# One column-tiled group for all logit sums of a block, and one pool of ten buffers for the products of both attention stages

## The chip, the cores and the metric

The kernel runs on one core of one Trainium2 chip. Its time is the device time of one execution in microseconds (us). A profiled execution has a span of its own, from its first to its last recorded instruction, which is a little shorter than the time of the run.

TensorE (PE) multiplies matrices, VectorE (DVE) does elementwise work and reductions, ScalarE (ACT) does functions and the copies from PSUM to SBUF, GpSimd (POOL) sets constants and takes powers, and SyncE (SP) issues all transfers.

## The reference

A transformer layer in which attention and feed-forward run side by side on the same normalised input: 2048 positions of 512 numbers, bf16.

```
xn  = layernorm(x)
out = x + A(xn) + B(xn)

A: q, k, v = xn @ wqkv, 32 heads of 16
   logits[h,s,w] = q[h,s] . k[h, s - 2*w] / 4     for w = 0..7 (masked below position 0)
   o[h,s] = sum over w of softmax(logits)[h,s,w] * v[h, s - 2*w]
   A = o @ wo
B: (gelu(xn @ w_gate) * (xn @ w_up)) @ w_down,    hidden width 1376
```

Each position looks at itself and at seven earlier ones, two apart. There is no dense product of queries and keys in it: logits are sums over 16 numbers of elementwise products, and so are the outputs over 8 weights.

## The kernel before

**Blocks.** The sequence is cut into four blocks of 512 positions, b = 0 to 3. For each block the kernel does, in this order of dependence: layer norm (L925 to L972) and a transpose of the result into `xnT`; the projections to q, k and v (L1045 for q and k of block 0, L1089 for the others; ACT copies them out at L1064, L1099, L1106, L1113); the logits; a softmax; the values' part; the feed-forward part (gate and up at L1305, gelu at L1315, the copy of up at L1322, their product on DVE at L1327 into `HT`); and the output (L1351 adds o @ wo, L1356 h @ w_down, in one PSUM bank; L1376 adds x).

**The logits.** The 512 channels are four groups g of 128, 8 heads each. For each g, DVE multiplies q by shifted keys, two times (wq = 0, 1), each for four of the eight shifts: a tensor of 128 x 2048 in bf16 (L1135), which goes to a buffer of the pool `PROD` (4 buffers of 4 KB per partition). TensorE then sums over the 16 channels of each head with a constant matrix `E8`: eight matmuls for one g (task `er`, L1151), each with 32 columns of weights, placed at `tile_position=(0, 32 * sj)`. That is the column-tiled mode, in which four matmuls of 32 columns stand side by side in the array. The windows of `E8` put each g on other rows, so that all four groups accumulate into one pair of PSUM banks (`lg`). The softmax (L1184 to L1214) starts when the fourth is done.

**The values' part.** The weights go through a scratch tensor in HBM (L1222 writes, L1229 reads into `PT`) and the values through another (L1120 writes, L1240 reads into `BS`). DVE multiplies them for each of four quarters dq in two halves (L1255), into the pool `PVS` (3 buffers of 8 KB, one for both halves). TensorE sums with the constant matrix `E4`, in the column-tiled mode as well, two quarters at a time: 16 matmuls (task `pvr`, L1274, `PVR_MERGE` = 2). ACT copies the sums to `OT` (L1285), which L1351 needs.

**The order of the work.** A planner writes it out before the kernel is built. Each task has an engine, a duration, what it reads and writes, and a priority (lower goes first). The planner goes through simulated time and gives each engine the most urgent task that is ready; it lets another task go first if that one fits in before. An item takes a buffer of its pool when its first task is placed, and gives it back when its last one is done. If no buffer is free, or the item's stream would be over its quota, the task can't be placed yet. The order of each engine is then fixed, and the engines wait for each other by semaphores. Lines that matter here:

```
sched = dict(PE_SLACK=1.6, DMA_BPUS=250e3,                         # L1387
             TOL=dict(pe=0.3, act=-0.3, dve=0.0, pool=-0.3, sp=0.0))
QUOTAS = dict(tp=2, qkv=2, lg=2, o=cfg.get("PVR_MERGE", 2), ffn=3, acc=2)   # L685
```

`PE_SLACK` is time that the planner leaves between the end of another engine's work and a TensorE task that waits for it. `QUOTAS` limits the PSUM banks (8 in all) by use. Feed-forward work has 3 banks, and four buffers each for the gate (`GG`) and up (`UU`) results, which come free when DVE has multiplied them (L1327). Priorities: logit products have base + 20 and value products base + 50, where base is 0, 700, 1400 and 2100 for the four blocks; feed-forward has 500 + 1000 b + j for its eleven column groups j. All transfers go through SP's one queue in planned order.

Of the kernel before, what the change touches and what calls it, by code (L numbers as in the profile page):

```python
# [638 lines left out]
BF = mybir.dt.bfloat16  # L639
# [24 lines left out]
def bass_parallel_sum__sliding_local_dilated__glu_gated_geglu__prompt_kernel(nc, A_x, A_wqkv, A_wo, B_x, B_w_gate, B_w_up, B_w_down, out, dbg=None, cfg=None):  # L664
    cfg = dict(cfg or {})
# [1 line left out]
    NSUBA = cfg.get("NSUBA", 1)  # L667
    NQT = cfg.get("NQT", 2)
    NXT = cfg.get("NXT", 3)
    NPROD = cfg.get("NPROD", 4)  # L670
    JA = cfg.get("JA", 8)
    NMS = cfg.get("NMS", 2)
    NDE = cfg.get("NDE", 1)
# [1 line left out]
    NPT = cfg.get("NPT", 2)  # L675
    NVT = cfg.get("NVT", 4)
    NBS = cfg.get("NBS", 3)
    NPVS = cfg.get("NPVS", 3)
    NOT = cfg.get("NOT", 2)
    NGG = cfg.get("NGG", 4)  # L680
    NHT = cfg.get("NHT", 2)
# [11 lines left out]
    PVR_MERGE = cfg.get("PVR_MERGE", 2)  # L693
# [11 lines left out]
    with contextlib.ExitStack() as es:  # L705
        block = es.enter_context(nc.Block())

        def sb(name, shape, dt):
            return es.enter_context(nc.sbuf_tensor(name, shape, dt))
# [10 lines left out]
        E8 = sb("E8", [128, 56], BF)  # L720
        E8f = sb("E8f", [128, 56], F32)
        E4 = sb("E4", [128, 32], BF)
# [11 lines left out]
        ms = sb("ms", [128, NMS, 3, 128], F32)  # L734
        XIN = sb("XIN", [128, NXIN, 2, 512], BF)
        QT = sb("QT", [128, NQT, 4, 512], BF)
        PROD = sb("PROD", [128, NPROD, 4, 512], BF)
        DE = sb("DE", [128, NDE, 1024], F32)
        PB = sb("PB", [128, NPB, 1024], BF)
        PT = sb("PT", [128, NPT, 1024], BF)  # L740
        VT = sb("VT", [128, NVT, 512], BF)
        BS = sb("BS", [128, NBS, 4, 514], BF)
        PVS = sb("PVS", [128, NPVS, 2, 4, 512], BF)
        OT = sb("OT", [128, NOT, 4, 512], BF)
        GG = sb("GG", [128, NGG, 512], BF)
        UU = sb("UU", [128, NGG, 512], BF)
# [3 lines left out]
        PS = es.enter_context(nc.psum_tensor("PS", [128, 4096], F32))  # L750
# [8 lines left out]
        G = Graph()  # L759
# [1 line left out]
        P_xin = Pool("xin", NXIN)  # L761
        P_xt = Pool("xt", NXT)
        P_qt = Pool("qt", NQT)
        P_prod = Pool("prod", NPROD)
        P_ms = Pool("ms", NMS)
        P_de = Pool("de", NDE)
        P_pb = Pool("pb", NPB)
        P_pt = Pool("pt", NPT)
        P_vt = Pool("vt", NVT)
        P_bs = Pool("bs", NBS)  # L770
        P_pvs = Pool("pvs", NPVS)
        P_ot = Pool("ot", NOT)
        P_gg = Pool("gg", NGG)
        P_uu = Pool("uu", NGG)
# [11 lines left out]
        I_E8 = Item("E8")  # L786
        I_E8f = Item("E8f")
        I_E4 = Item("E4")
# [21 lines left out]
            out=cf[:, :], in_=cf[:, :], pattern=[[-1, 128]], compare_op=ALU.is_equal, fill=0.0, base=0,  # L810
            channel_multiplier=1), rd=[I_cf], wr=[I_cf], prio=PC)
        G.task("pool", "c_idb", 0.65, lambda e: e.tensor_copy(out=ident[:, :], in_=cf[:, :]),
               rd=[I_cf], wr=[I_ident], prio=PC)
# [87 lines left out]
        for p in range(NP):  # L901
            b = p // 2
# [123 lines left out]
        for b in range(NB):  # L1026
# [98 lines left out]
                                   wr=[(I_VD, (b, g, hf))], prio=hb + 13, nbytes=128 * HWD * 2)  # L1125

            it_lg = Item("lg%d" % b, P_ps, "lg", width=2)
            for g in range(4):
                prs = []
                for wq in range(2):  # L1130
                    it_pr = Item("pr%d_%d_%d" % (b, wq, g), P_prod, "p")
                    prs.append(it_pr)

                    def mk_p(wq=wq, g=g, it=it_pr, itq=it_qt, c0b=c0b):
                        return lambda e: e.tensor_tensor(  # L1135
                            out=PROD[:, it.slot, :, :],
                            in0=bass.AP(QT, (itq.slot * 4 + g) * 512, [[NQT * 4 * 512, 128], [0, 4], [1, 512]]),
                            in1=bass.AP(KT, g * PITCH + 16 + c0b - 12 - 2 * wq, [[4 * PITCH, 128], [4, 4], [1, 512]]),
                            op=ALU.mult)
                    rdk = [(I_KT, (0, "t", t)) for t in range(4)] if b == 0 else [(I_KT, (b, g, 0))]  # L1140
                    rdk.append((I_KT, "pad") if b == 0 else (I_KT, (0, "t", 3)) if b == 1 else (I_KT, (b - 1, g, 0)))
                    rdq = [(it_qt, ("t", t)) for t in range(4)] if b == 0 else [(it_qt, (g, 0))]
                    G.task("dve", "pr%d_%d_%d" % (b, wq, g), d_dve(2048, 0.52), mk_p(),
                           rd=rdq + rdk, wr=[it_pr], prio=base + 20)

                def mk_r(g=g, prs=prs, lg=it_lg):
                    def f(e):
                        ins = None
                        for wq in range(2):
                            for sj in range(4):  # L1150
                                ins = e.matmul(  # L1151
                                    PS[32 * sj:32 * sj + 32, 512 * (lg.slot + wq):512 * (lg.slot + wq) + 512],
                                    lhsT=E8[:, 24 - 8 * g:56 - 8 * g],
                                    rhs=PROD[:, prs[wq].slot, :, sj * 128:(sj + 1) * 128],
                                    start=(g == 0), stop=(g == 3), tile_position=(0, 32 * sj))
                        return ins
                    return f
                G.task("pe", "er%d_%d" % (b, g), 0.46, mk_r(),
                       rd=prs + [I_E8] + ([it_lg] if g > 0 else []), wr=[it_lg], prio=base + 5, mode="c",
                       util=0.8)  # L1160

            it_pt = Item("pt%d" % b, P_pt, "pt")
            it_de = Item("de%d" % b, P_de, "de")
# [68 lines left out]
                   prio=base + 37, nbytes=256 * 1024)  # L1232

            it_ot = Item("ot%d" % b, P_ot, "ot")
            pvr_grp = []
            for dq in range(4):
                it_bs = Item("bs%d_%d" % (b, dq), P_bs, "bs")
                for j in (0, 2, 1, 3):
                    def mk_l(j=j, dq=dq, it=it_bs, c0b=c0b):
                        return lambda e: e.dma_start(  # L1240
                            BS[32 * j:32 * j + 32, it.slot, :, :],
                            bass.AP(VD, dq * 128 * PITCH + 16 + c0b - 2 - 4 * (3 - j),
                                    [[PITCH, 32], [32 * PITCH, 4], [1, 514]]))
                    rdv = [(I_VD, (b, g, hf)) for g in range(4) for hf in range(NHALF[b])]
                    if b > 0:
                        rdv += [(I_VD, (b - 1, g, NHALF[b - 1] - 1)) for g in range(4)]
                    else:
                        rdv.append((I_VD, "pad"))
                    G.task("sp", "ldb%d_%d_%d" % (b, dq, j), 0, mk_l(), rd=rdv, wr=[(it_bs, j)],
                           prio=base + 45, nbytes=int(1.8 * 32 * 4 * 514 * 2))  # L1250
                it_pv = Item("pv%d_%d" % (b, dq), P_pvs, "pv")
                for half in range(2):
                    def mk_pv(half=half, it=it_bs, ito=it_pv, itp=it_pt):
                        o = 2 - 2 * half
                        return lambda e: e.tensor_tensor(  # L1255
                            out=bass.AP(PVS, (ito.slot * 2 + half) * 2048,
                                        [[NPVS * 4096, 128], [512, 4], [128, 4], [1, 128]]),
                            in0=bass.AP(BS, it.slot * 4 * 514 + o,
                                        [[NBS * 4 * 514, 128], [514, 4], [128, 4], [1, 128]]),
                            in1=bass.AP(PT, itp.slot * 1024 + half * 128,  # L1260
                                        [[NPT * 1024, 128], [0, 4], [256, 4], [1, 128]]),
                            op=ALU.mult)
                    G.task("dve", "pv%d_%d_%d" % (b, dq, half), d_dve(2048, 0.52), mk_pv(),
                           rd=[it_bs, it_pt], wr=[(it_pv, half)], prio=base + 50)
                it_o = Item("o%d_%d" % (b, dq), P_ps, "o")
                pvr_grp.append((dq, it_pv, it_o))
                if len(pvr_grp) == PVR_MERGE:
                    def mk_pr(grp=list(pvr_grp)):
                        def f(e):
                            ins = None  # L1270
                            for (dq_, itp, it) in grp:
                                for half in range(2):
                                    for d4 in range(4):
                                        ins = e.matmul(PS[32 * d4:32 * d4 + 32, 512 * it.slot:512 * it.slot + 512],  # L1274
                                                       lhsT=E4[:, :], rhs=PVS[:, itp.slot, half, d4, :],
                                                       start=(half == 0), stop=(half == 1),
                                                       tile_position=(0, 32 * d4))
                            return ins
                        return f
                    G.task("pe", "pvr%d_%d" % (b, dq), PVR_MERGE * 0.56 + 0.0, mk_pr(),  # L1280
                           rd=[g_[1] for g_ in pvr_grp] + [I_E4], wr=[g_[2] for g_ in pvr_grp],
                           prio=base + 7, mode="c")
                    for (dq_, itp_, it_) in pvr_grp:
                        def mk_eo(dq=dq_, it=it_, ito=it_ot):
                            return lambda e: e.activation(  # L1285
                                out=OT[:, ito.slot, dq, :], in_=PS[:, 512 * it.slot:512 * it.slot + 512],
                                func=ACTF.Identity)
                        G.task("act", "evo%d_%d" % (b, dq_), d_act(512), mk_eo(), rd=[it_], wr=[(it_ot, dq_)],
                               prio=base + 52)
                    pvr_grp = []  # L1290
# [162 lines left out]
```

## Time and profile before

| | |
|---|---|
| time, three runs | 201.35 us (201.34 to 201.56) |
| span of the profiled execution | 199.7 us (that run took 201.42) |
| TensorE busy | 194.4 us, 97% |
| DVE busy | 149.2 us, 75% |
| ACT busy | 104.7 us, 52% |
| logit products, L1135 | 32 of 1216 ns |
| value products, L1255 | 32 of 1216 ns |
| logit sums, L1151 | 128 matmuls in 16 groups |
| value sums, L1274 | 128 matmuls in 8 groups |

Busy time is counted from the start of an instruction to its end; matmuls overlap, so that the mean of one (380 ns) is not what one costs in a row of them. What a step costs at its place is read from the chain of work that ended last: each line is a stretch of the chain, with its start, its length, the engine and the line of the code, and the number of instructions. In a timeline the entry in brackets is the idle time of the engine before the row and what ended it. In a list of waits the columns are the total, the number of times and the longest.

### The profile page before, as it was taken

To read this page: it belongs to the slowest core of one execution; us is meant where nothing else is said; L and a number is where in the kernel's file an instruction comes from. 1 tells how busy PE (TensorE), PEld (TensorE's weight loads), DVE (VectorE), ACT (ScalarE), POOL (GpSimd) and SP (SyncE) were. 2 spreads that over 40 slices of the span, in tenths; PEclk is the share of its full clock that TensorE was granted. 3 is DMA by queue.
4 is the path that set the end of the run, shared out by engine and by line. 5 is a ranking of instruction groups with operands and counts; after the bars stand their busy time and mean duration, and the time that the engine had idled before them with its cause. 6 is when DMAs were issued, how large, how long until landed. Compare 5 with 4: busy or idle time off the path is not lost.

```text
span 199.7 us, 3150 instructions
## 1 busy us (share of the span) xinstructions
PE 194.4 (97%) x1192; PEld 89.5 (45%) x1192; DVE 149.2 (75%) x230; ACT 104.7 (52%) x171; POOL 10.4 (5%) x32
## 2 busy tenths in 40 slices
PE   7899999999999999998999999999999999999994
PEld 2694344444443444443344444333444444444483
DVE  3889999889998997699996529999792986222231
ACT  4477469775667302677563036874892007767000
POOL 6520010101000010000000000000000000000000
PEclk9999999999999999999999999999999999999999
DMA  5999998898659426355931244377112440010121
GB/s 146 360 402 375 276 102 170 210 256 144 184 144 218 50 93 144 119 141 151 216 76 53 82 133 105 95 163 167 53 38 67 119 121 26 0 53 5 37 81 41
DMA packets 33055, 27.03 MB, mean 135 GB/s; under 512 B 9392, under 2 KB 31504, under 8 KB 33040
## 3 DMA queue, kind: packets, MB, share of 16 engines
q1 hardware_dynamic: 33040, 26.83, 53.8%
q8 instruction: 9, 0.15, 0.3%
q14 instruction: 6, 0.05, 0.1%
HBM read 19.99 MB, written 5.26 MB: 126 GB/s over the span
## 4 chain that ended last, share of the span: by engine, by line
PE 93%; DMA 2%; ACT 2%; DVE 1%; SPq 1%; issue 0%; DVEq 0%
PE PS L1305 37%; PE PS L1356 19%; PE PS L1089 17%; PE PS L1351 7%; PE PS L1151 4%; PE PS L1274 4%; PE PS L1045 3%; DMA XIN<-in_A_x_dram 2%; ACT L1315 1%; ACT OT L1285 1%; ACT UU L1322 0%; PE PS L997 0%; SPq L910 0%; DVE st L925 0%; ACT GG L1315 0%
## 5 line engine op out<-in xcount | busy, mean ns | idle before, releaser
L1305 PE MATMUL PS<-xnT,Wu 128*128 128x512 bf16 (+1 forms) x176 | 45.2, 380 | 0.0
L1305 PE MATMUL PS<-xnT,Wg 128*128 128x512 bf16 (+1 forms) x176 | 45.1, 379 | 0.0
L1356 PE MATMUL PS<-Wd,HT 128*128 128x512 bf16 (+3 forms) x198 | 41.3, 356 | 0.0
L1255 DVE TENSOR_TENSOR PVS<-BS,PT 128x2048 bf16<-128x2048 bf16 x32 | 37.1, 1216 | 4.2 <-DMA PT<-pt_scratch 3.5
L1135 DVE TENSOR_TENSOR PROD<-QT,KT 128x2048 bf16<-128x2048 bf16 x32 | 36.9, 1216 | 0.5 <-ACT KT L1106 0.3
L1089 PE MATMUL PS<-xnT,Wqkv 128*128 128x512 bf16 x160 | 35.9, 379 | 0.0
L1315 ACT ACTIVATE GG<-PS 128x512 bf16<-128x512 f32 (+1 forms) x44 | 26.5, 602 | 15.5 <-PE PS L1305 11.8
L1322 ACT ACTIVATE UU<-PS 128x512 bf16<-128x512 f32 (+1 forms) x44 | 26.5, 602 | 9.8 <-PE PS L1305 9.5
L1327 DVE TENSOR_TENSOR HT<-GG,UU 128x512 bf16<-128x512 bf16 (+1 forms) x44 | 17.2, 417 | 15.5 <-ACT UU L1322 15.5
L1356 PEld LDWEIGHTS PS<-Wd,HT 128*128 128x128 bf16 (+1 forms) x198 | 19.4, 98 | 18.7
L1305 PEld LDWEIGHTS PS<-xnT,Wg 128*128 128x128 bf16 (+1 forms) x176 | 17.1, 100 | 21.6 <-issue 2.5
L1305 PEld LDWEIGHTS PS<-xnT,Wu 128*128 128x128 bf16 (+1 forms) x176 | 16.6, 100 | 22.9 <-issue 3.4
L1376 DVE TENSOR_TENSOR OB<-PS,XR 128x512 bf16<-128x512 f32 (+1 forms) x18 | 11.3, 628 | 19.7 <-PE PS L1356 18.5
L1089 PEld LDWEIGHTS PS<-xnT,Wqkv 128*128 128x128 bf16 x160 | 15.4, 98 | 19.0 <-issue 0.4
L1351 PE MATMUL PS<-Wo,OT 128*128 128x512 bf16 (+1 forms) x72 | 16.8, 355 | 0.0
L1285 ACT ACTIVATE OT<-PS 128x512 bf16<-128x512 f32 x16 | 8.7, 595 | 15.3 <-PE PS L1274 15.3
L1106 ACT ACTIVATE KT<-PS 128x512 bf16<-128x512 f32 x12 | 7.2, 597 | 13.3 <-PE PS L1089 13.3
L1099 ACT ACTIVATE QT<-PS 128x512 bf16<-128x512 f32 x12 | 7.2, 596 | 12.8 <-PE PS L1089 12.6
L925 DVE BATCH_NORM_STATS2 st<-XIN 128x6 f32<-128x512 bf16 x16 | 10.7, 685 | 3.7 <-DMA XIN<-in_A_x_dram 3.7
L1113 ACT ACTIVATE VT<-PS 128x512 bf16<-128x512 f32 x16 | 9.6, 598 | 4.7 <-PE PS L1089 4.7
L942 POOL TENSOR_TENSOR sq<-ve,mhalf 128x2 bf16<-128x2 f32 (+1 forms) x10 | 6.7, 666 | 68.5 <-DVE ve L936 68.5
L1351 PEld LDWEIGHTS PS<-Wo,OT 128*128 128x128 bf16 x72 | 6.9, 97 | 7.2 <-issue 0.4
(53 smaller groups left out, 117.1 us busy)
## 6 DMA issues: line engine op xcount, KB each, us to landing
BS<-vt_scratch SPq DMA_DIRECT2D x64, 128.5 KB, 3.1
vt_scratch<-VT SPq DMA_DIRECT2D x16, 128.0 KB
XR<-in_A_x_dram SPq DMA_DIRECT2D x16, 128.0 KB, 2.1
XIN<-in_A_x_dram SPq DMA_DIRECT2D x7, 256.0 KB, 6.1
out_dram<-OB SPq DMA_DIRECT2D x14, 128.0 KB, 2.0
Wqkv<-in_A_wqkv_dram SPq DMA_DIRECT2D x3, 512.0 KB, 4.2
Wg<-in_B_w_gate_dram SPq DMA_DIRECT2D x1, 1376.0 KB
Wu<-in_B_w_up_dram SPq DMA_DIRECT2D x1, 1376.0 KB, 11.2
```

Of the source, the lines that this page charges most:

```text
L925: return lambda e: e.bn_stats(out=st[:, t, :], in_=XIN[:, it.slot, t2, :])
L1089: ins = e.matmul(PS[:, 512 * it.slot:512 * it.slot + HWD], lhsT=lhsT, rhs=xnT[:, itx.slot, kt, c0:c0 + HWD], start=(kt == 0), stop=(kt == 3))
L1135: return lambda e: e.tensor_tensor(out=PROD[:, it.slot, :, :], in0=bass.AP(QT, (itq.slot * 4 + g) * 512, [[NQT * 4 * 512, 128], [0, 4], [1 ...
L1255: return lambda e: e.tensor_tensor(out=bass.AP(PVS, (ito.slot * 2 + half) * 2048, [[NPVS * 4096, 128], [512, 4], [128, 4], [1, 128]]), in0 ...
L1285: return lambda e: e.activation(out=OT[:, ito.slot, dq, :], in_=PS[:, 512 * it.slot:512 * it.slot + 512], func=ACTF.Identity)
L1305: ins = e.matmul(PS[0:M, 512 * it.slot:512 * it.slot + 512], lhsT=Wx[:, kt, j * 128:j * 128 + M], rhs=xnT[:, itx.slot, kt, :], start=(kt = ...
L1315: return lambda e: e.activation(out=GG[0:M, ito.slot, :], in_=PS[0:M, 512 * it.slot:512 * it.slot + 512], func=ACTF.Gelu_apprx_tanh)
L1322: return lambda e: e.activation(out=UU[0:M, ito.slot, :], in_=PS[0:M, 512 * it.slot:512 * it.slot + 512], func=ACTF.Identity)
L1327: return lambda e: e.tensor_tensor(out=HT[0:M, ito.slot, j, :], in0=GG[0:M, ig.slot, :], in1=UU[0:M, iu.slot, :], op=ALU.mult)
L1351: ins = e.matmul(PS[:, 512 * it.slot:512 * it.slot + CW], lhsT=OT[:, ito.slot, dq, ti * 128:(ti + 1) * 128], rhs=Wo[:, dq, c0:c1], start=( ...
L1356: ins = e.matmul(PS[:, 512 * it.slot:512 * it.slot + CW], lhsT=HT[0:K, ith.slot, j, ti * 128:(ti + 1) * 128], rhs=Wd[0:K, j, c0:c1], start ...
L1376: return lambda e: e.tensor_tensor(out=OB[:, ito.slot, 0:CW], in0=PS[:, 512 * it.slot:512 * it.slot + CW], in1=XR[:, itx.slot, c0:c1], op= ...
```

## The change

All four logit groups of a block become one: `er` is issued once, with 32 matmuls, and waits for the eight products of the block. `PROD` and `PVS` are replaced by one pool `UNI` of ten buffers of 4 KB, which is the same memory. A value product takes one buffer for each half, where it took half of a double one. The first logit product of a block takes the buffers for all eight products at once, and the first value product of a pair of quarters takes those for all four. Each of the two streams may hold at most eight buffers.

```diff
-    NPROD = cfg.get("NPROD", 4)
+    NUNI = cfg.get("NUNI", 10)
+    ER_MERGE = cfg.get("ER_MERGE", 4)
-    NPVS = cfg.get("NPVS", 3)
...
+        P_uni = Pool("uni", NUNI, quotas=cfg.get("UNI_Q", dict(p=8, pv=8)))
...
+            er_grp = []
+            pr_items = [[Item("pr%d_%d_%d" % (b, wq, g), P_uni, "p") for wq in range(2)] for g in range(4)]
             for g in range(4):
...
-                           rd=rdq + rdk, wr=[it_pr], prio=base + 20)
+                           rd=rdq + rdk, wr=[(it_pr, "d")] + ([(q, "a") for gg in range(g, g + ER_MERGE) for q in pr_items[gg]
+                                                      if q is not it_pr] if g % ER_MERGE == 0 and wq == 0 else []),
+                           prio=base + 20)
+                er_grp.append((g, prs))
+                if len(er_grp) < ER_MERGE:
+                    continue
...
-                        for wq in range(2):
-                            for sj in range(4):
+                        for (g, prs) in grp:
+                            for wq in range(2):
+                                for sj in range(4):
...
-                G.task("pe", "er%d_%d" % (b, g), 0.46, mk_r(),
-                       rd=prs + [I_E8] + ([it_lg] if g > 0 else []), wr=[it_lg], prio=base + 5, mode="c",
-                       util=0.8)
+                G.task("pe", "er%d_%d" % (b, g), 0.432 * ER_MERGE + 0.1, mk_r(),
+                       rd=[q for g_ in er_grp for q in g_[1]] + [I_E8] + ([it_lg] if g >= ER_MERGE else []),
+                       wr=[it_lg], prio=base + 5, mode="c", util=0.8)
+                er_grp = []
...
+            pv_items = [[Item("pv%d_%d_%d" % (b, dq, half), P_uni, "pv") for half in range(2)] for dq in range(4)]
...
-                           rd=[it_bs, it_pt], wr=[(it_pv, half)], prio=base + 50)
+                           rd=[it_bs, it_pt], wr=[(it_pv[half], "d")] + ([(q, "a") for dd in range(dq, dq + PVR_MERGE) for q in pv_items[dd]
+                                                      if q is not it_pv[half]]
+                                                     if dq % PVR_MERGE == 0 and half == 0 else []), prio=base + 50)
```

More of the change, by code (lines that the diff above doesn't have):

```diff
@@ L736, in bass_parallel_sum__sliding_local_dilated__glu_gated_geglu__prompt_kernel @@
         QT = sb("QT", [128, NQT, 4, 512], BF)
-        PROD = sb("PROD", [128, NPROD, 4, 512], BF)
+        UNI = sb("UNI", [128, NUNI, 4, 512], BF)
         DE = sb("DE", [128, NDE, 1024], F32)
@@ L742, in bass_parallel_sum__sliding_local_dilated__glu_gated_geglu__prompt_kernel @@
         BS = sb("BS", [128, NBS, 4, 514], BF)
-        PVS = sb("PVS", [128, NPVS, 2, 4, 512], BF)
         OT = sb("OT", [128, NOT, 4, 512], BF)
@@ L763, in bass_parallel_sum__sliding_local_dilated__glu_gated_geglu__prompt_kernel @@
         P_qt = Pool("qt", NQT)
-        P_prod = Pool("prod", NPROD)
+        P_uni = Pool("uni", NUNI, quotas=cfg.get("UNI_Q", dict(p=8, pv=8)))
         P_ms = Pool("ms", NMS)
@@ L770, in bass_parallel_sum__sliding_local_dilated__glu_gated_geglu__prompt_kernel @@
         P_bs = Pool("bs", NBS)
-        P_pvs = Pool("pvs", NPVS)
         P_ot = Pool("ot", NOT)
@@ L1130, in bass_parallel_sum__sliding_local_dilated__glu_gated_geglu__prompt_kernel @@
                 for wq in range(2):
-                    it_pr = Item("pr%d_%d_%d" % (b, wq, g), P_prod, "p")
+                    it_pr = pr_items[g][wq]
                     prs.append(it_pr)
@@ L1135, in mk_p @@
                         return lambda e: e.tensor_tensor(
-                            out=PROD[:, it.slot, :, :],
+                            out=UNI[:, it.slot, :, :],
                             in0=bass.AP(QT, (itq.slot * 4 + g) * 512, [[NQT * 4 * 512, 128], [0, 4], [1, 512]]),
@@ L1143, in bass_parallel_sum__sliding_local_dilated__glu_gated_geglu__prompt_kernel @@
                     G.task("dve", "pr%d_%d_%d" % (b, wq, g), d_dve(2048, 0.52), mk_p(),
-                           rd=rdq + rdk, wr=[it_pr], prio=base + 20)
-                def mk_r(g=g, prs=prs, lg=it_lg):
+                           rd=rdq + rdk, wr=[(it_pr, "d")] + ([(q, "a") for gg in range(g, g + ER_MERGE) for q in pr_items[gg]
+                                                      if q is not it_pr] if g % ER_MERGE == 0 and wq == 0 else []),
+                           prio=base + 20)
+                er_grp.append((g, prs))
@@ L1147, in f, with mk_r @@
+                if len(er_grp) < ER_MERGE:
+                    continue
+                def mk_r(grp=list(er_grp), lg=it_lg):
                     def f(e):
                         ins = None
-                        for wq in range(2):
-                            for sj in range(4):
[L1151 to L1155, printed above, removed]
@@ L1156, in f @@
-                        return ins
-                    return f
-                G.task("pe", "er%d_%d" % (b, g), 0.46, mk_r(),
-                       rd=prs + [I_E8] + ([it_lg] if g > 0 else []), wr=[it_lg], prio=base + 5, mode="c",
-                       util=0.8)
+                        for (g, prs) in grp:
+                            for wq in range(2):
+                                for sj in range(4):
+                                    ins = e.matmul(
+                                        PS[32 * sj:32 * sj + 32, 512 * (lg.slot + wq):512 * (lg.slot + wq) + 512],
+                                        lhsT=E8[:, 24 - 8 * g:56 - 8 * g],
+                                        rhs=UNI[:, prs[wq].slot, :, sj * 128:(sj + 1) * 128],
+                                        start=(g == 0), stop=(g == 3), tile_position=(0, 32 * sj))
@@ L1250, in bass_parallel_sum__sliding_local_dilated__glu_gated_geglu__prompt_kernel, with mk_pv @@
                            prio=base + 45, nbytes=int(1.8 * 32 * 4 * 514 * 2))
-                it_pv = Item("pv%d_%d" % (b, dq), P_pvs, "pv")
+                it_pv = pv_items[dq]
                 for half in range(2):
-                    def mk_pv(half=half, it=it_bs, ito=it_pv, itp=it_pt):
+                    def mk_pv(half=half, it=it_bs, ito=it_pv[half], itp=it_pt):
                         o = 2 - 2 * half
                         return lambda e: e.tensor_tensor(
-                            out=bass.AP(PVS, (ito.slot * 2 + half) * 2048,
-                                        [[NPVS * 4096, 128], [512, 4], [128, 4], [1, 128]]),
+                            out=bass.AP(UNI, ito.slot * 2048,
+                                        [[NUNI * 2048, 128], [512, 4], [128, 4], [1, 128]]),
                             in0=bass.AP(BS, it.slot * 4 * 514 + o,
@@ L1274, in f @@
                                         ins = e.matmul(PS[32 * d4:32 * d4 + 32, 512 * it.slot:512 * it.slot + 512],
-                                                       lhsT=E4[:, :], rhs=PVS[:, itp.slot, half, d4, :],
+                                                       lhsT=E4[:, :], rhs=UNI[:, itp[half].slot, d4, :],
                                                        start=(half == 0), stop=(half == 1),
@@ L1280, in bass_parallel_sum__sliding_local_dilated__glu_gated_geglu__prompt_kernel @@
                     G.task("pe", "pvr%d_%d" % (b, dq), PVR_MERGE * 0.56 + 0.0, mk_pr(),
-                           rd=[g_[1] for g_ in pvr_grp] + [I_E4], wr=[g_[2] for g_ in pvr_grp],
+                           rd=[q for g_ in pvr_grp for q in g_[1]] + [I_E4], wr=[g_[2] for g_ in pvr_grp],
                            prio=base + 7, mode="c")
```

## The prediction

> **What bounds the kernel now.** I read the page's first part first (which engine is full), then its slices (is it full all the time), then the chain of work that ended last in order of time (what one step costs at its place), the waits, and the DVE timeline.
>
> ```profile
> PE 194.4 (97%) x1192; PEld 89.5 (45%) x1192; DVE 149.2 (75%) x230; ACT 104.7 (52%) x171; POOL 10.4 (5%) x32
> ...
> PE   7899999999999999998999999999999999999994
> ...
> DVE  3889999889998997699996529999792986222231
> ...
> PE 93%; DMA 2%; ACT 2%; DVE 1%; SPq 1%; issue 0%; DVEq 0%
> ```
>
> TensorE is busy in every slice but the first ones (loads, layer norm) and the last. The chain is 93% TensorE, so whatever shortens the TensorE stream shortens the kernel, as long as nothing makes it wait. DVE is near full from slice 3 to slice 27 and then slack: two thirds of the kernel has little DVE time to give.
>
> What one visit to the column-tiled mode costs is in the chain (columns: start us, us, what):
>
> ```profile
> 18.53 0.86 PE PS L1305 x4
> 19.39 0.55 PE PS L1151 x8
> 19.93 1.83 PE PS L1305 x8
> 21.77 0.55 PE PS L1151 x8
> ...
> 37.54 3.45 PE PS L1305 x16
> ...
> 53.73 0.98 PE PS L1274 x16
> ...
> 60.65 0.98 PE PS L1274 x16
> 61.62 0.43 PE PS L1151 x8
> ```
>
> Sixteen full matmuls take 3.45 us, so 8 take 1.725. Next to a logit group (L1151, column-tiled) the same 8 take 1.83, and the group takes 0.55. Directly behind another column-tiled group (61.62) the same 8 logit matmuls take 0.43; and 16 product-sum matmuls (L1274) take 0.98, which is 0.55 + 0.43. So a visit costs 0.12 us in and 0.105 us out, 0.225 together, however many matmuls it holds. The same shows from start to start: 21.77 less 19.39 is 2.38, against 1.725 + 0.43 = 2.155.
>
> The waits of TensorE and of the engines that feed it:
>
> ```profile
> DVE PVS L1255 <- DMA PT<-pt_scratch: 3.5, 2, 1.9
> ...
> PE PS L1274 <- ACT UU L1322: 0.5, 1, 0.5
> ```
>
> After the start TensorE loses half a microsecond in all. The DVE timeline shows how products of the two stages now mix:
>
> ```profile
> 42.62 3.50 DVE L1135 TENSOR_TENSOR PROD<-QT,KT 128x2048 bf16<-128x2048 bf16 x3
> ...
> 46.58 6.89 DVE L1255 TENSOR_TENSOR PVS<-BS,PT 128x2048 bf16<-128x2048 bf16 x6
> 53.40 2.35 DVE L1135 TENSOR_TENSOR PROD<-QT,KT 128x2048 bf16<-128x2048 bf16 x2
> ...
> 79.90 1.23 DVE L1135 TENSOR_TENSOR PROD<-QT,KT 128x2048 bf16<-128x2048 bf16 x1 [0.30 <-ACT KT L1106]
> ...
> 83.05 6.90 DVE L1255 TENSOR_TENSOR PVS<-BS,PT 128x2048 bf16<-128x2048 bf16 x6 [1.85 <-DMA PT<-pt_scratch]
> ```
>
> Logit products of block 1 start at 42.62, value products of block 0 cut in at 46.58. Hold on to this: the new pool forbids it.
>
> **What the Trainium skill says.** "TensorEngine Tiling (Array Packing)", Key Properties: changing the tiling mode drains TensorE. The trace agrees and prices it at 0.225 us for in and out. "TensorE: Matmul & The Clock Gate", Back-to-back issue gap: N/2.4 + 2.5 ns, 215.8 ns for N=512; the trace has 3.45 us / 16 = 215.6 ns. Same page, Part 3 (Packing small matmuls): column tiles run at the same time; here 8 of them cost 0.43 us, two slots of 0.216, so four share a slot. Same page, Architectural detail: VectorE is a strict FIFO; so a DVE product that waits for a buffer holds all DVE work behind it. In the trace the group list gives PVS 0.7 us of such waiting for L1274.
>
> **The change, part by part.**
>
> *Logit groups.* Before, 16 logit groups of 8 matmuls; after, 4 of 32, with the same 128 matmuls. Count visits from the PE timeline. Of the 16 logit groups, 14 stand between full matmuls on both sides, and two (61.45 and 94.03) follow a product-sum group directly and share its visit. With 8 product-sum groups that is 22 visits. After: 4 + 8 = 12, or fewer. Gone: 10 x 0.225 = 2.25 us. Each merged group should take 0.12 + 4 x 0.43 = 1.84 us.
>
> *Where it starts.* A merged group needs all 8 products of its block. Block 0: products end at 24.83; the planner keeps 1.6 us of slack before a PE task that waits on another engine, so about 26.5 to 28.3, where now the last group starts at 26.46 and ends at 27.0. The softmax of block 0 (mask, L1190) moves from 27.1 to about 28.4. DVE has HT multiplies (L1327, 417 ns each) to do meanwhile, so I take zero for this; bounds 0 and 1.3 us of a chain that isn't the end of anything. TensorE in 18.4 to 26.5 must do FFN groups (0.863 each) in place of logits: 9.4 of them. With no HT multiply done, the 4 GG and 4 UU buffers and 3 PSUM banks hold 11. It fits.
>
> *PSUM.* The pair of banks for logits is held from the merged group on, instead of from the first of four: some 7 us less per block. A gain in freedom, costed at nothing (TensorE waited 0.5 us in all, so it can't give more).
>
> *The shared pool.* Memory is the same: 4 x 4 KB + 3 x 8 KB before, 10 x 4 KB after. The first logit product takes all 8 buffers of its block; the first value product of a pair takes 4. As 8 + 4 is over 10, products of the two stages can never be in flight together. On each change of stage DVE waits for the TensorE group that empties the pool: 1.84 (or 0.98) plus the 1.6 of slack, some 2.6 to 3.4 us, in which only other DVE work runs (HT, layer norm, softmax). Queued behind the waiting product are all later DVE tasks, among them HT multiplies that free GG and UU, hence ACT evictions, hence FFN banks. On SP, the BS loads wait for value products (7.3 us in SP's waits) and stores and transposes queue behind them; their number does not change.
>
> *Which stage goes first.* At 42.62 the value products of block 0 were not ready in the planner's eyes and a logit product filled the hole. The same hole will be there, and that product now takes 8 buffers at once. Then: 8 products at 1.146 (9.17/8 in the timeline) plus 0.5 of layer norm, 42.6 to 52.3; logits 53.9 to 55.8; value products 55.8 to 65.0; second product-sum group at 66.7 to 67.7; OT at 68.3; first output matmul (L1351) about 68.8, now at 64.43. From about 50.4, when QKV of block 1 is done, TensorE has 18.4 us less 2.0 (1.84 + 0.105 on leaving) and 2.2 (two of 0.98 + 0.105) for column groups: 14.2/0.863 = 16.5 FFN groups of block 1. Of these, 11 may pass without a HT multiply and 3 more for the one or two done around 53 to 55.8: about 14 up to 65. Needed up to 65: (14.6 - 2.0 - 1.1)/0.863 = 13.3. So the fit is close, and the 2 to 3 groups after 65 hang on HT multiplies being let in before or between softmax steps. Bounds: 0, and 2 groups, 1.7 us. I take 0.1. At the next block the hole was one product wide (79.90). If it recurs, the first output matmul of block 1 moves from 102.8 to about 107.5, with FFN of blocks 1 and 2 as filler: again 0 to 1.7, taken as 0.1. Block 3 has a slack of 14 us between its last product-sum group (169) and its output (184): 0.
>
> *Sum.* 199.7 - 2.25 + 0.2 = 197.65 of the profiled span. The timed runs stand 1.65 above the span (201.35 against 199.7; the profiled run itself was 201.42): **199.3 us**.
>
> **Rivals.**
> 1. *Not faster: DVE becomes the gate at both changes of stage* (50 to 69 and 88 to 108). Late value products delay OT while HT multiplies are held up, GG and UU fill, and TensorE stands. For: DVE is over 90% in these slices, ACT already waited 2.5 us once for HT. Against: from 103 to 165 DVE is busy for 47.3 of 62 us, so 14.7 us are free to catch up in, and the planner sees all buffers. Price 1.7 to 3 at each: 199.1 + 2 x 1.9 = 202.9. It decides against the change from 2.65 us of TensorE idle time on.
> 2. *One such stall*, eating the gain: 199.1 + 2 = 201.1.
> 3. *The switch is not saved*: the four E8 windows in one group could each cost a drain of their own, so that nothing changes. Against it: 0.43 at 61.62, and L1151 already loads weights for each matmul (x128). 201.3.
> 4. *More*: logits land next to a product-sum group in two blocks (0.45) and the 0.5 us wait goes: 199.1 less 0.95 is 198.2.
>
> **How the numbers follow.** Forecast as worked 0.53 (199.0 to 200.5); rival 4 0.08; rivals 2 and 3 together 0.13; rival 1 0.26. No change means within 0.2%, 0.4 us (200.95 to 201.75), about what these runs can tell. Faster: 0.61 plus the mild end of rival 2, 0.64. Same: 0.10. Slower: 0.26. The range 198.3 to 203.0 leaves out about half of rival 1 above and half of rival 4 below, some 0.17.
>
> **What would show it.** Right: four logit steps of about 1.84 us in the chain, TensorE busy time some 2 us less, PROD and PVS products (now one tile) in unbroken runs of 8, full blocks by stage. Wrong: TensorE waits for GG, UU or HT in the waits, a digit under 9 in the middle slices, or a logit group over 2.2 us.

## The result, and the profile after

The changed kernel takes 199.33 us (198.96 to 199.59, four runs), the kernel before beside it 201.45 us. The ratio is 0.989 with a 95% interval of 0.987 to 0.991: 1.1% faster. The forecast was 199.3. The size is right; the sum behind it had errors that cancel, so that a part of the hit is luck. The experiments show which part.

The page of the changed kernel, first part, slices, and the chain by engine:

```profile
span 197.7 us, 3146 instructions
...
PE 191.9 (97%) x1192; PEld 91.3 (46%) x1192; DVE 149.1 (75%) x230; ACT 105.0 (53%) x171; POOL 11.4 (6%) x32
...
PE   7799999999999999999999999999999999999993
...
DVE  3789989999989999999879379995692986122131
...
PE 94%; DMA 3%; DVE 1%; SPq 1%; issue 0%; DVEq 0%
```

TensorE is still the bound, with no slice below 9 between the start and the end: the 8 at slice 18 is gone. Its busy time fell by 2.5 us with the same 1192 matmuls. ACT has left the chain.

The chain in order of time (start us, us, what), around the merged logit groups, now L1158, and the value sums, now L1285:

```profile
26.82 1.84 PE PS L1158 x32
...
56.40 1.84 PE PS L1158 x32
58.24 1.83 PE PS L1316 x8
...
88.16 1.84 PE PS L1158 x32
...
98.95 0.12 issue
99.07 1.05 PE PS L1285 x16
...
136.97 1.84 PE PS L1158 x32
```

Each merged group takes 1.84 us, which is 0.12 + 4 x 0.43 as forecast, and the eight matmuls behind one take 1.83, the same 0.105 on leaving as before. Twelve visits to the column-tiled mode are left: these four and eight of L1285.

DVE's timeline of the changed kernel (both stages now write UNI; L1135 are logit products, L1264 value products):

```profile
42.50 8.03 DVE L1135 TENSOR_TENSOR UNI<-QT,KT 128x2048 bf16<-128x2048 bf16 x7
50.45 2.35 DVE L1264 TENSOR_TENSOR UNI<-BS,PT 128x2048 bf16<-128x2048 bf16 x2
52.72 1.22 DVE L1135 TENSOR_TENSOR UNI<-QT,KT 128x2048 bf16<-128x2048 bf16 x1
...
58.29 4.63 DVE L1264 TENSOR_TENSOR UNI<-BS,PT 128x2048 bf16<-128x2048 bf16 x4 [0.47 <-PE PS L1158]
```

This contradicts the prediction. At 50.45 two value products run while the eight logit products of block 1 still hold their buffers; the logit sums come at 56.40. The stages do share the pool, as 8 + 2. The reason is in the code: only the *first* product of a group asks for all of the group's buffers. The planner couldn't place the first value product (it needs four, two were free), but the others of the group don't depend on it and ask for one buffer each, so two of them went ahead; in the experiment that adds this dependence none does. Between blocks 1 and 2 it is the same: value products at 83.29 and 85.03, and the last logit product at 86.16.

### The profile page after: what moved, and what is told of

It is laid out like the page before. It is cut to its first block, busy times and chain, and to the rows that moved or that the text cites. A ratio compares the mean times of both kernels' runs of the same rounds, so it can differ in the third digit from the quotient of the medians.

```text
span 197.7 us, 3146 instructions
## 1 busy us (share of the span) xinstructions
PE 191.9 (97%) x1192; PEld 91.3 (46%) x1192; DVE 149.1 (75%) x230; ACT 105.0 (53%) x171; POOL 11.4 (6%) x32
## 4 chain that ended last, share of the span: by engine, by line
PE 94%; DMA 3%; DVE 1%; SPq 1%; issue 0%; DVEq 0%
PE PS L1316 39%; PE PS L1367 19%; PE PS L1087 18%; PE PS L1362 7%; PE PS L1285 4%; PE PS L1158 4%; PE PS L1043 3%; DMA XIN<-in_A_x_dram 3%; PE PS L995 0%; SPq L908 0%; DVE st L923 0%; SPq L860 0%; DVE OB L1387 0%; DVE XIN L970 0%; DVE rstd L946 0%
## 5 line engine op out<-in xcount | busy, mean ns | idle before, releaser
L1316 PE MATMUL PS<-xnT,Wu 128*128 128x512 bf16 (+1 forms) x176 | 44.6, 379 | 0.0
L1316 PE MATMUL PS<-xnT,Wg 128*128 128x512 bf16 (+1 forms) x176 | 44.4, 379 | 0.0
L1264 DVE TENSOR_TENSOR UNI<-BS,PT 128x2048 bf16<-128x2048 bf16 x32 | 37.5, 1219 | 2.9 <-DMA PT<-pt_scratch 1.7
L1135 DVE TENSOR_TENSOR UNI<-QT,KT 128x2048 bf16<-128x2048 bf16 x32 | 37.2, 1219 | 0.5 <-PE PS L1285 0.2
L1316 PEld LDWEIGHTS PS<-xnT,Wu 128*128 128x128 bf16 (+1 forms) x176 | 17.4, 100 | 21.0 <-issue 0.8
L940 POOL TENSOR_TENSOR sq<-ve,mhalf 128x2 bf16<-128x2 f32 (+1 forms) x10 | 7.6, 763 | 77.7 <-DVE ve L934 77.7
L1214 DVE TENSOR_REDUCE ms<-DE 128x128 f32<-128x1024 f32 x4 | 7.6, 1908 | 2.6 <-ACT DE L1209 2.6
```

Source lines behind the costliest of these rows:

```text
L1135: return lambda e: e.tensor_tensor(out=UNI[:, it.slot, :, :], in0=bass.AP(QT, (itq.slot * 4 + g) * 512, [[NQT * 4 * 512, 128], [0, 4], [1, ...
L1264: return lambda e: e.tensor_tensor(out=bass.AP(UNI, ito.slot * 2048, [[NUNI * 2048, 128], [512, 4], [128, 4], [1, 128]]), in0=bass.AP(BS, ...
L1316: ins = e.matmul(PS[0:M, 512 * it.slot:512 * it.slot + 512], lhsT=Wx[:, kt, j * 128:j * 128 + M], rhs=xnT[:, itx.slot, kt, :], start=(kt = ...
```

## The experiments

The rival to the visits is that the new pool, or the new order that the planner made with it, brings the gain. The second question is what sharing costs. All ratios below are to the kernel before, timed beside each group of experiments (201.85 us in both groups).

### The visits alone, in the same order of work

The planned order of the changed kernel is kept; the four parts of each logit group are emitted with one matmul of the next feed-forward group behind each (what that group waits for is waited for ahead of the first part).

```diff
+            if t.name.startswith("er"):
+                skip = t2 = self.order[eng_name][i + 1]
...
+                for k in range(4):
+                    fa.part(e, k).then_inc(t.sem, 1) if k == 3 else fa.part(e, k)
+                    ins = fb.part(e, k)
+                ins.then_inc(t2.sem, 1)
...
```

> The changed kernel with the planned order of all engines kept, but each merged logit group is cut into its four parts again and the four matmuls of the next feed-forward group are put one behind each part, so that TensorE enters the column-tiled mode 12 more times. If the gain is the price of visits (0.225 us each), this gives back 12 x 0.225 = 2.7 us: about 202.0, slower than the kernel before by 0.3%. If the gain came from the pool or from the new order of the work, it stays near 199.4.

Measured: 202.19 us, ratio 1.001 (1.000 to 1.003). The whole gain is given back. TensorE's timeline of this kernel:

```profile
26.65 0.62 PE L1171 MATMUL PS<-UNI,E 128*32 128x512 bf16 x8
27.20 0.39 PE L1330 MATMUL PS<-xnT,Wu 128*128 128x512 bf16 x1
27.52 0.61 PE L1171 MATMUL PS<-UNI,E 128*32 128x512 bf16 x8
...
101.83 1.05 PE L1299 MATMUL PS<-UNI,E 128*32 128x512 bf16 x16 [0.61 <-DVE UNI L1278]
```

From start to start the cycle is 27.52 - 26.65 = 0.87 us for eight column-tiled matmuls (0.43) and one full one (0.216): 0.22 us for the visit, with as little as a single full matmul between two visits. Twelve of them are 2.64 us; the ratios of the two kernels differ by 0.0125 (0.0144 with the repeat of the change further down), which is 2.5 to 2.9 us. In the profiled execution, which took 202.83 us, the TensorE stream is 3.5 us longer than in the changed kernel: the visits, and 0.9 us more of waits, the longest the one above. The softmax of block 1 starts at 68.2 us here and at 66.05 in the changed kernel, which is the likely reason of these waits; that was not tested. Most executions took less, so the agreement of the times is good to half a microsecond and not better.

### Half the merge, with two separate pools

```diff
-    ER_MERGE = cfg.get("ER_MERGE", 4)
+    ER_MERGE = cfg.get("ER_MERGE", 2)
+    NPA = cfg.get("NPA", 4)
...
-        P_uni = Pool("uni", NUNI, quotas=cfg.get("UNI_Q", dict(p=8, pv=8)))
+        P_prod = Pool("prod", NPA)
+        P_pvs = Pool("pvs", NUNI - NPA)
...
```

> Two logit groups in one (8 in the kernel in place of 4 or 16), and two separate pools as before: 4 buffers for logit products, 6 single ones for value products. 16 visits in the planned order against 23 that paid before. Visits theory: 7 x 0.225 = 1.6 us less than before, about 199.8. Theory that the shared pool brings the gain: no gain, about 201.4.

Measured: 199.45 us, ratio 0.988 (0.987 to 0.990), as fast as the change itself. The pool isn't needed for the gain. The page's slices of this kernel:

```profile
PE   7799999999999999999999999999999999999994
```

There is no wait in the middle. The kernel is 2.4 us faster than the one before, where 1.6 was expected: the waits around slice 18, which the expectation had left in, are gone too.

One thing doesn't fit. With 16 visits against 12 it should be 0.9 us slower than the change, and the times don't show that. Its TensorE stream is longer, by 0.66 us (table further down); but before and after the stream its profile has some 0.7 us less than that of the change, and why is open.

### Half the merge, with the shared pool

The edit is the first pair of lines above alone.

> Two logit groups in one, with the shared pool of ten. The planned order has 15 visits. Visits theory: 8 x 0.225 = 1.8 us less than before, about 199.6. Theory that the shared pool makes the stages wait for each other (rival 1 of the prediction): slower than the one with separate pools by more than 0.5 us, with TensorE waiting in the middle.

Measured: 202.76 us, ratio 1.004 (1.003 to 1.006): slower than before, 3.3 us slower than with separate pools. Slices, and rows of TensorE's timeline:

```profile
PE   7699999999999999999999699999999999999994
```

```profile
102.88 1.05 PE L1285 MATMUL PS<-UNI,E 128*32 128x512 bf16 x16 [0.44 <-DVE UNI L1264]
...
112.28 0.82 PE L1367 MATMUL PS<-Wd,HT 128*128 128x512 bf16 x3 [1.80 <-DVE HT L1338]
```

The output sums of block 1 waited 1.80 us for the last HT multiply, which stood on DVE behind products and softmax steps (105.13 to 111.81). Sharing does cost, in some orders of work: the mechanism that rivals 1 and 2 name exists.

### The shared pool alone

```diff
-    ER_MERGE = cfg.get("ER_MERGE", 4)
+    ER_MERGE = cfg.get("ER_MERGE", 1)
```

> The shared pool alone: ten buffers for both stages, but 16 logit groups of 8 matmuls as before. The planned order has 21 visits against 23 that paid. Visits theory with a free pool: 0.45 us less than before, about 201.0. If the pool itself saves time (wait of TensorE at 92 gone): 200.5. If sharing costs: over 202.

Measured: 201.95 us, ratio 1.000 (0.999 to 1.001). The pool by itself brings nothing. One visit fewer (21 against 22, counted below) is lost in waits of TensorE, the longest 0.39 us for HT and two of some 0.17 for products.

### The exclusion that the prediction took for granted

```diff
+                    if g % ER_MERGE == 0 and wq == 0:
+                        t_first = t_pr
+                    else:
+                        G.order_after(t_pr, t_first)
...
+                    if dq % PVR_MERGE == 0 and half == 0:
+                        t_firstv = t_pv
+                    else:
+                        G.order_after(t_pv, t_firstv)
```

> The changed kernel, but the other products of a group are planned only after the one that takes the group's buffers, so that no product slips in with a buffer of its own: the two stages can then really never hold buffers together, as the prediction had it. 12 visits, as in the changed kernel. Prediction's sum (exclusion costs 0.2 us): about 199.4. Its rival 1 (DVE becomes the gate at both changes of stage): 201 to 203, with waits of TensorE in the middle.

Measured: 202.14 us, ratio 1.001 (1.000 to 1.003): all of the gain is gone. TensorE's waits of the middle, from its timeline:

```profile
97.92 1.04 PE L1324 MATMUL PS<-xnT,Wg 128*128 128x512 bf16 x4 [0.29 <-DVE DE L1207]
...
102.13 1.04 PE L1324 MATMUL PS<-xnT,Wg 128*128 128x512 bf16 x4 [0.58 <-ACT GG L1334]
...
105.88 1.02 PE L1370 MATMUL PS<-Wo,OT 128*128 128x512 bf16 x4 [1.85 <-DVE HT L1346]
```

and DVE's and ACT's timelines just before:

```profile
85.96 6.90 DVE L1268 TENSOR_TENSOR UNI<-BS,PT 128x2048 bf16<-128x2048 bf16 x6
93.11 2.36 DVE L1268 TENSOR_TENSOR UNI<-BS,PT 128x2048 bf16<-128x2048 bf16 x2 [0.26 <-DMA BS<-vt_scratch]
95.39 1.22 DVE L1202 TENSOR_REDUCE ms<-PS 128x128 f32<-128x1024 f32 x1
96.64 1.23 DVE L1207 TENSOR_TENSOR DE<-PS,ms 128x1024 f32<-128x1024 f32 x1
97.78 1.42 DVE L1346 TENSOR_TENSOR HT<-GG,UU 128x512 bf16<-128x512 bf16 x4
```

```profile
96.72 1.08 ACT L1304 ACTIVATE OT<-PS 128x512 bf16<-128x512 f32 x2 [2.75 <-PE PS L1293]
97.82 1.28 ACT L1213 ACT_TABLE_LOAD   x1
99.11 1.06 ACT L1213 ACTIVATE DE<-DE 128x1024 f32<-128x1024 f32 x1
100.19 1.28 ACT L1334 ACT_TABLE_LOAD   x1
```

From 85.96 to 97.78 DVE does no HT multiply: eight value products in a row and two softmax steps. ACT's four copies of up results from 86.71 to 91.89 fill the four buffers, and TensorE's further results stay in PSUM. The first wait ends when a softmax step frees the banks of the logits. By the time the buffers come free ACT is at the exp and its two table loads (3.6 us), and the second wait ends with the gelu behind them. The third ends with an HT multiply that stood behind three more softmax steps (101.26 to 105.32). It is 0.29 + 0.58 + 1.85 = 2.72 us of idle time in all, at one change of stage, between blocks 1 and 2.

### Twelve buffers, not shared

```diff
-    NUNI = cfg.get("NUNI", 10)
-    NPA = cfg.get("NPA", 4)
-    ER_MERGE = cfg.get("ER_MERGE", 2)
+    NUNI = cfg.get("NUNI", 12)
+    NPA = cfg.get("NPA", 8)
+    ER_MERGE = cfg.get("ER_MERGE", 4)
...
-    NBS = cfg.get("NBS", 3)
-    NOT = cfg.get("NOT", 2)
+    NBS = cfg.get("NBS", 2)
+    NOT = cfg.get("NOT", 1)
```

(Against the kernel with half the merge and separate pools.)

> Full merge (4 logit groups) with two separate pools, 8 buffers for logit products and 4 for value products; the 8 KB more come from one OT buffer in place of two and two BS buffers in place of three. 10 visits in the planned order. If sharing ten buffers still costs the changed kernel something, and by visits alone (2 x 0.225 = 0.45 us), this is about 198.9 or less. If the missing OT and BS buffers make DVE or TensorE wait: over 199.8.

Measured: 199.29 us, ratio 0.987 (0.985 to 0.989), not to be told from the change (0.987 in the same comparison). Ten visits were expected, for 0.45 us less than the change. Ten there are, but one logit group has a gap before it:

```profile
103.10 0.98 PE PS L1287 x16
104.08 0.09 issue
104.17 1.91 PE PS L1160 x32
...
133.19 0.98 PE PS L1287 x16
134.16 1.73 PE PS L1160 x32
```

At 134.16 a logit group follows a value group without a gap: 1.73, four times 0.43, no entry to pay. At 104.17 there is a gap of 0.09 us and the group takes 1.91. That is no entry either: the group waited for its last product, which ended on DVE at 104.03. From start to start the value group and the logit group are 1.14 us apart, where the pair at 133.12 and 133.99 is 0.87 apart. So the wait cost 0.27, more than the 0.22 that the shared visit saved. To gain from sharing a visit, the second group's products must be ready.

### The value sums of a block in one group too

```diff
-    PVR_MERGE = cfg.get("PVR_MERGE", 2)
+    PVR_MERGE = cfg.get("PVR_MERGE", 4)
```

The share of PSUM banks for these sums (`o` in `QUOTAS`) goes from 2 to 4 with it.

> The changed kernel, with the value sums of a block in one group too (32 matmuls, 4 PSUM banks). 8 visits against 12: by visits alone 4 x 0.225 = 0.9 us less than the changed kernel, about 198.4. If eight value products at once hold the shared pool too long, or four PSUM banks are missing elsewhere: 199.4 or more.

Measured: 198.53 us, ratio 0.982 (0.980 to 0.984). It beats both kernels: 0.91 us, 0.5%, below the change in the same comparison, where 0.9 was expected. Chain:

```profile
69.56 1.84 PE PS L1285 x32
...
102.06 1.91 PE PS L1285 x32
```

### The change once more

> The changed kernel once more, beside the others of this call. Visits theory and prediction: 199.3, a ratio of 0.989 to the kernel before. The span's first transposition (8.40 us in the profile, 7.87 before) and its tail should vary from profile to profile with the first loads, with no bearing on the change.

Measured: 199.44 us, ratio 0.987 (0.985 to 0.989). In its profile TensorE's chain starts at 8.51 us and 2.98 lie behind its end; in the first profile of the change it was 8.40 and 2.96, before the change 7.87 and 2.64. So the longer start and end came back, and this repeat doesn't bear out that they vary without the change.

## Why the prediction was right, point by point

**The price of a visit**, 0.225 us, was right, and the first experiment measures it by itself (0.22). All ten profiles agree. Take TensorE's stream from the first matmul of the chain to the end of the last, less the waits inside it. A wait is read from start to start: how much later than usual a matmul begins after the one before it. Usual is 0.216 us after a full matmul of 512 columns and 0.31 at a change of mode (twice 0.09 more, and 0.03 in the steps between, is the price again). In four traces some records of matmuls are missing; a step of two slots was taken for one of them.

| kernel | visits | stream, us | waits in it | less waits |
|---|---|---|---|---|
| split visits | 24 | 189.83 | 1.12 | 188.71 |
| before | 22 | 189.19 | 0.87 | 188.32 |
| shared pool alone | 21 | 189.39 | 1.25 | 188.14 |
| half merge, separate pools | 16 | 187.00 | 0.04 | 186.96 |
| half merge, shared pool | 15 | 189.67 | 2.86 | 186.81 |
| change | 12 | 186.34 | 0.23 | 186.11 |
| change once more | 12 | 186.20 | 0.09 | 186.11 |
| exclusion | 12 | 189.46 | 3.38 | 186.08 |
| twelve separate | 10 | 186.01 | 0.35 | 185.66 |
| value sums merged too | 8 | 185.41 | 0.17 | 185.24 |

From 22 to 8 visits it is 3.08 us, 0.22 for each, and no kernel lies more than 0.05 us off this line.

The Trainium skill ("TensorEngine Tiling (Array Packing)", Key Properties) says that changing the mode drains the array, and these steps agree. On the step of 215.6 ns, which the prediction set beside "Back-to-back issue gap", that section gives the formula for a matmul by itself and 131 ns for a stream with weight loads; the stream measured here has 215.6.

**The count** of ten visits was right. The expectations of the experiments speak of 23 visits that paid before, because the group at 94.03, which the prediction took as sharing a visit, takes 0.61 us in the chain where the one at 61.62 takes 0.43. But what it shows is a wait. TensorE's timeline of both pairs, and DVE's, before the change:

```profile
60.58 1.05 PE L1274 MATMUL PS<-PVS,E 128*32 128x512 bf16 x16
61.45 0.60 PE L1151 MATMUL PS<-PROD,E 128*32 128x512 bf16 x8
...
92.89 1.05 PE L1274 MATMUL PS<-PVS,E 128*32 128x512 bf16 x16 [0.46 <-ACT UU L1322]
94.03 0.61 PE L1151 MATMUL PS<-PROD,E 128*32 128x512 bf16 x8
```

```profile
92.67 8.03 DVE L1135 TENSOR_TENSOR PROD<-QT,KT 128x2048 bf16<-128x2048 bf16 x7
```

The first of these seven products ends 1.21 us after its start, at 93.88, and the group that needs it starts at 94.03, 1.14 us behind the value group in place of 0.87. It waited 0.27 us for the product, of which the chain shows 0.09 as a gap.

**The waits that were there before** are the term that was too small. The prediction saw one, 0.5 us, gave its end a chance of 0.08 as part of rival 4, and left it out of the sum. From start to start it is 0.53, with the 0.27 above and two of some 0.03 it is 0.87, and 0.23 is left in the change. With 2.2 for the visits that makes 2.86; the stream is 189.19 - 186.34 = 2.85 shorter.

**The pool** is the step that failed. The prediction said that the two stages can never be in flight together, and that this costs 0.1 us at each of two changes of stage. The premise was wrong (8 + 2 at 50.45), and so was the price: with real exclusion it is 2.72 us of idle time at one change of stage, and at the other nothing. That is the form of rival 2, one stall, at more than its 2 us, and by itself just over the 2.65 that rival 1 named. Had the code worked as it was read, there would have been no gain, and the forecast would have been some 2.4 us too low (1.001 against 0.989 of the kernel before). In the change itself TensorE waits 0.23 us.

**What hid the surplus.** 2.85 less in the stream became 2.0 in the span (199.7 to 197.7). In the changed kernel's profile TensorE's chain starts at 8.40, not 7.87, since the first load of x took 4.99 us and not 4.46; and from the end of the stream to the end of the span, mostly the last store, it is 2.96 and not 2.64 us. Neither is explained, and whether the change causes it is open. The load took 4.9 to 5.2 us in all profiles of kernels with the full merge, 4.46 in that of before, 4.61 and 4.65 in two others, and 5.22 in the one with half the merge and the shared pool, though the first 19 transfers are issued in the same order in all of them. The tail is 2.6 to 3.0 us; it is close to 3.0 in five of the six with the full merge, but 2.7 in the one with exclusion and 3.0 in the half merge with the shared pool.

So the forecast sum (2.05 us) met the span (2.0) for two reasons that cancel. It had 0.64 us of waits too few and an allowance for the pool (0.2) too much, 0.84 in all; and a start and an end that came out 0.85 us longer were not in it. That these two meet is luck. The price and the number of visits, which carry the forecast, are not.

**Confirmed as forecast:** the merged group at 1.84 us; the logits of block 0 at 26.8 (forecast 26.5) without harm; no wait of TensorE for the later softmax.

**Dates and readings that were off.** The first output matmul of block 0 came at 70.87 us, not 68.8, and that of block 1 at 102.84, not 107.5; TensorE waited before neither. DVE's slices were read as near full from 3 to 27 and as over 90% at both changes of stage. Counted from 0, slices 21 to 23 have 6, 5 and 2 in that line, and slice 12, in the first change, has 8. The sum doesn't rest on this.

## What to carry to other kernels

Where TensorE is the bound, count how often it goes in and out of the column-tiled mode and multiply by what one visit costs in the trace (0.22 us here); merge the groups, and where two of those that stay share a visit, see that the second one's input is ready: a wait of 0.27 us there cost more than the visit. Read waits from start to start, since the idle time in a profile is less. Before you price a limit on buffers, check which instruction asks for them: a group that "takes all at once" does so only if its first member has to come first. A change of buffers that brings nothing by itself can lose more than the merge saves, and what it starves is not the engine that waits for the buffers but the small multiplies queued behind.

## What the runs showed of the hardware that was not expected

- One full matmul between two column-tiled groups is enough for the whole price: 0.22 us, with 0.32 us between the groups in the chain.
- The price doesn't depend on how much a visit holds: from 24 to 8 visits, of 8 to 48 matmuls, the stream without its waits changes by 0.22 us for each.
- Idle time of TensorE in the profile is less than what a wait costs, because the record of a matmul (0.38 us) reaches past the usual start of the next (0.216): 0.09 shown for 0.27 within the column-tiled mode, 0.46 for 0.53 at a change of mode, 1.85 for 2.01 within the full mode.
